# Attention and a gated feed-forward on one core: another start-up list, gate sums out of a projection, and another last tile

## The chip, the core and the metric

One core of a Trainium2 chip runs the program. TensorE (PE) multiplies matrices and loads the weights for that (PEld), VectorE (DVE), ScalarE (ACT) and GpSimd (POOL) work on vectors, SyncE (SP) issues most transfers. The metric is the time of one execution on the device in microseconds (us).

## What is computed

```python
x = A_x                                   # 1 x 2048 x 512
g = sigmoid((x * gate_w).sum(-1))         # one gate for each token
# attention: 32 heads of 16, one K and one V for all heads
q = (x @ wq) as 32 heads;  k = x @ wk;  v = x @ wv
a = softmax(q k^T / 4) v, heads side by side, @ wo
# feed-forward of width 1792
b = ((x @ w_gate) * (x @ w_up)) @ w_down
out = g * a + (1 - g) * b
```

All is float32. Where a product of 32-bit accuracy is wanted, a matrix is kept as a high and a low part in fp32r, and each product is three matmuls (`mm3`): high by high, low by high, high by low.

## The kernel before

**Units and rounds.** Attention works in 64 units: 128 tokens (a tile `t` of a chunk `c` of 512 tokens) by eight heads (a group `g`). A unit has 16 steps in each of three passes. The first pass (`p1`, L699) multiplies Q by K with the queries on the partitions, and DVE takes the maximum of each row (L700); two matmuls to a step, one for each half of the heads, on the upper and the lower 64 rows of TensorE at the same time (two lanes, LANE = 232 ns in the planner). After the last maximum of a unit, `p1_end` reduces them on DVE (L708 to L714), stores them through DRAM (L720, four transfers) and fetches them as two more rows of the unit's Q tile (L727, two transfers). The second pass (`p2`, L740) needs these rows: it gives the scores less the maximum, transposed, and ACT takes the exponential (L741). The third (`pv`, L753) multiplies by V in four column tiles of 32, and ACT copies the sum out (L757), once for each unit.

**The planner.** The schedule is manual: the order in which Python emits the instructions is the order on each engine, and each engine runs its own in order. A string of 144 letters, `ORDER`, is one round of 16 steps: `a`, `b` issue a `p1` matmul on the two lanes, `c`, `d` a `p2` matmul, `p` two steps of `pv`, and `e`, `f` (36 each) a matmul of a filling job, at twelve to a job, so three jobs a round. The jobs are the Q projections of the groups (`q_jobs`), the feed-forward's products (`ffn_job`, `down_jobs`) and the output projection by `wo` (in `norm`), 198 in all. `APART` is the round used instead where a down-projection job of two feed-forward tiles stands ready; there are two such jobs to a chunk. A class `State` keeps estimated times; `later` and `at` put an action (a DMA, a copy) at an estimated time.

**The front.** Before the rounds stand hand-ordered calls (L766 to L798): `x_trans0` and `x_trans` transpose x by TensorE and split it, `kv` projects K and V (a stationary matrix of 128 columns that holds wk three times and wv), `v_trans` brings V back, one Q projection (chunk 0, group 0) is done, stored (`q_store`, two transfers) and fetched (`q_fetch`, L226, six transfers to a unit). `steps` puts four `p1` steps between them. The gate sums are 16 products on POOL (`gate_sum`, L320), each summed on ACT (L324), planned from the end of the front on. Then comes the lead: until 25 `p1` steps (LEAD) are issued and six jobs (LEADJOBS) are filled, `p1` steps and jobs alternate; then `ORDER` runs 64 times. Of unit 0 all 16 steps come first in `order1`, then unit 1, and so on.

**The end.** After the last `pv`, ACT copies the sum to `osb`; TensorE multiplies three quarters of the last tile by `wo` (nine matmuls, 512 columns); `picks` has built two selecting matrices, and eight matmuls by them (L672) take the sums and the values out of `osb` into one bank; DVE forms the reciprocal (L675) and the product (L677); a split, three more matmuls and one VectorE operation (L354) finish the tile, and one transfer stores it (L367).

Of the kernel before, what the change touches and what calls it, by code (L numbers as in the profile page):

```python
# [48 lines left out]
LEADJOBS = 6  # L49
# [12 lines left out]
SLOT = 1  # L62
HALVES = (slice(0, 64), slice(64, 128))
# [5 lines left out]
def mix_kernel(ctx: ExitStack, tc: tile.TileContext, x, wq, wk, wv, wo, wg, wu, wd, gw, out):  # L69
# [34 lines left out]
    z = consts.tile([128, NC * NT], F32, name="z")  # L104
# [58 lines left out]
    def load_x(c):  # L163
        if c < 2:
            xn = [w512("y", F32, 8) for _ in range(NT)]
        else:
            pairs = [work.tile([128, 2, 512], F32, name="P", tag="P", bufs=PBUF) for _ in range(2)]
            xn = [t[:, i] for t in pairs for i in range(2)]
        for t in range(NT):
            eng = nc.scalar if c == 0 and t == NT - 1 else nc.sync  # L170
            eng.dma_start(xn[t], x2[c * 512 + t * 128:c * 512 + t * 128 + 128, :])
        return xn
# [33 lines left out]
    def q_store(c, g, qh, ql):  # L206
        dq[c, g] = []
        for src in (qh, ql):
            d = dram.tile([128, 512], F32, name="dq", tag="dq", bufs=2 * NC * NG)
            nc.sync.dma_start(d, src.bitcast(F32))  # L210
            dq[c, g].append(d)
        dqat[c, g] = clock["T"] + 4500.0
# [5 lines left out]
    def q_fetch(u):  # L218
        c, g, t = units[u]
        q = Q[u] = work.tile([128, 4, 128], F32R, name="Q", tag="Q", bufs=QB)  # L220
        for d, rows in zip(dq[c, g], ((0, 32), (16,))):
            for half in range(2):
                for r in rows:
                    b = half * 64 + r
                    src = d[half * 64:half * 64 + 64, t * 128:(t + 1) * 128]
                    nc.sync.dma_start(q[b:b + 16].bitcast(F32), src.rearrange("(s d) q -> d s q", d=DH))  # L226
        qat[u] = clock["T"] + 6000.0

    kvn = work.tile([128, 4, 32], F32, name="kvn", tag="oT", bufs=2)
    nc.scalar.dma_start(kvn[:, :, 0:16], wk_v)  # L230
    nc.scalar.dma_start(kvn[:, :, 16:32], wv_v)
    xns = {0: load_x(0)}
    wqn = [stage(wq_v[:, :, 0:128])]
    xns[1] = load_x(1)
    xns[2] = load_x(2)
    xns[3] = load_x(3)
    wqs = [[w512("wh", F32R, WB), w512("wl", F32R, WB)] for g in range(NG)]
    kvs2 = [work.tile([128, 4, 32], F32R, name=n, tag=n, bufs=2) for n in ("rb", "raw")]
# [4 lines left out]
    def kv_split():  # L243
# [8 lines left out]
        split2(*wqs[0], wqn[0])  # L252

    def x_trans0():
        xT[0] = x_tiles()
        hi, lo = xT[0][2:]
        for t in range(NT):
            p = bank(2 + t, "px")
            for k in range(4):
                nc.tensor.transpose(p[:, KS[k]], xns[0][t][:, KS[k]], ident)  # L260
            split(hi[:, :, KS[t]], lo[:, :, KS[t]], p.rearrange("p (k q) -> p k q", k=4))
            if t == 1:
                kv_split()

    def x_trans(c, ks=range(4), pool=()):
        xn = xns[c]
        if c not in xT:
            xT[c] = [[w[:, k] for k in range(4)] for w in (woh, wol)] if c == 3 else \
                x_tiles((("hh", "hl"), ("wdh", "wdl"))[c - 1])
        for k in ks:  # L270
            p = bank(2 + (4 * c + k) % 5, "px")
            for t in range(NT):
                nc.tensor.transpose(p[:, KS[t]], xn[t][:, KS[k]], ident)  # L273
            if k in pool:
                xs = w512(("yt", "osb")[k % 2], F32, 2)
                nc.scalar.copy(xT[c][0][k], p)
                nc.scalar.copy(xs, p)
                nc.gpsimd.tensor_tensor(xT[c][1][k], xs, xT[c][0][k].bitcast(F32), op=OP.subtract)
            else:
                split(xT[c][0][k], xT[c][1][k], p)  # L280

    kvs = {}

    def kv(c, between=None):
        p = ms_bank(c % 2)
# [3 lines left out]
        mm_all(p, prods[:6], True, False)  # L289
        if between:  # L290
            between()
        mm_all(p, prods[6:], False, True)
        Kc = KK[:, c * 512:(c + 1) * 512]
        kvs[c] = w512("gs", F32, 3)
        nc.scalar.activation(Kc, p, AF.Identity, bias=kneg)
        nc.vector.scalar_tensor_tensor(Kc, Kc.bitcast(F32), klow, p, op0=OP.mult, op1=OP.add)
        nc.scalar.copy(kvs[c], p)

    def v_trans(c):
        pv = bank(7, "pv")  # L300
        for t in range(4):
            nc.tensor.transpose(pv[:, t * 128:(t + 1) * 128], kvs[c][:, t * 128:(t + 1) * 128], ident)  # L302
        nc.vector.tensor_copy(V[:, c * 4:(c + 1) * 4, 0:DH].rearrange("p t (h d) -> p t h d", h=2),
                              pv.rearrange("p (t h c) -> p t h c", t=4, h=2)[:, :, :, 50:58])
# [8 lines left out]
    gate_left = [(c, t) for c in (2, 3, 0, 1) for t in range(NT)]  # L313

    def gate_sum():
        if not gate_left:
            return
        c, t = gate_left.pop(0)
        scr = w512("yt", F32, 2)
# [336 lines left out]
    def picks():  # L656
# [4 lines left out]
        for t in sels:  # L661
            nc.gpsimd.memset(t, 0.0)
# [338 lines left out]
```

## Time and profile before

| what | us |
|---|---|
| median of 3 runs (lowest to highest) | 1620.87 (1620.53 to 1621.84) |
| the profiled execution | 1621.27 |
| its span, first to last instruction | 1619.5 |
| PE busy in it | 1610.8 |
| DVE busy | 1381.0 |
| ACT busy | 1245.7 |
| POOL busy | 744.7 |

The granted TensorE clock was 0.999 over the span. Matmuls overlap, so a busy PE is not one at its peak; what bounds a stage is read from what ended the waits there. In a timeline line stand the start, the length, the engine, the line of the kernel, the operation, the tiles written and read, the count, and in brackets the idle time before with what ended it. In the chain of waits stand start, length and what the time went to.

### The profile page before, as it was taken

The page shows a single profiled execution, that of the slowest core. Times are in us where ns is not written, and L with a number is a line of the kernel's source. Part 1 is how long each engine was busy: PE and PEld are TensorE (multiplying, and loading weights), DVE is VectorE, ACT ScalarE, POOL GpSimd, SP SyncE. Part 2 cuts the span into 40 slices and gives each one's busy share as a digit, 9 for nine tenths or more (in the row PEclk, how much of TensorE's full clock was granted, in tenths as well). Part 3 has the DMA queues.
Part 4 walks back from the last instruction along what each step waited for, and adds up shares of the span by engine and source line. Part 5 has one row for each costly group of instructions (what it writes and reads, how often), then busy time and mean ns, then how long its engine had stood idle before and what let it go on. Part 6 is the DMA issues. An engine that isn't in the chain of part 4 may idle for free.

```text
span 1619.5 us, 35319 instructions
## 1 busy us (share of the span) xinstructions
PE 1610.8 (99%) x13126; PEld 1042.4 (64%) x13126; DVE 1381.0 (85%) x2410; ACT 1245.7 (77%) x2411; POOL 744.7 (46%) x876
## 2 busy tenths in 40 slices
PE   9999999999999999999999999999999999999998
PEld 7666666666666666666666666576566666666664
DVE  6988888888898888888888888888888898898870
ACT  4787777777788787787778787787788787787785
POOL 5515652624644642635443651643743641642732
PEclk9999999999999999999999999999999999999999
DMA  4463322212312221212231221222231221222101
GB/s 161 174 212 114 97 67 59 61 54 72 102 58 72 66 73 54 65 52 69 64 100 62 71 66 57 64 59 65 62 111 52 68 79 53 62 65 60 36 25 38
DMA packets 184991, 121.44 MB, mean 75 GB/s; under 512 B 46196, under 2 KB 154356, under 8 KB 184820
## 3 DMA queue, kind: packets, MB, share of 16 engines
q1 hardware_dynamic: 183620, 118.87, 24.5%
q8 instruction: 103, 1.69, 0.4%
q14 instruction: 68, 0.56, 0.1%
q10 hardware_dynamic: 1200, 0.33, 0.1%
HBM read 82.96 MB, written 36.17 MB: 74 GB/s over the span
## 4 chain that ended last, share of the span: by engine, by line
PE 97%; DVE 1%; ACT 1%; issue 0%; POOL 0%; POOLq 0%; ACTq 0%
PE ms L872 34%; PE acc L753 29%; PE s L740 18%; PE s L699 15%; DVE mx L700 1%; PE ms L150 1%; ACT P L741 1%; PE px L273 0%; PE wo L150 0%; PE warm L764 0%; ACT yt L361 0%; PE pv L302 0%; PE pick L672 0%; PE px L260 0%; DVE rb L675 0%
## 5 line engine op out<-in xcount | busy, mean ns | idle before, releaser
L700 DVE TENSOR_REDUCE mx<-s 128x1 f32<-128x512 f32 x2048 | 1306.9, 684 | 171.2 <-PE s L699 87.9
L741 ACT ACTIVATE P<-s 128x512 f32<-128x512 f32 x2048 | 1077.9, 605 | 257.1 <-PE s L740 188.0
L740 PE MATMUL s<-Q,KK 50*128 50x512 f32 x2048 | 750.3, 411 | 0.1
L699 PE MATMUL s<-KK,Q 48*128 48x512 f32 x2048 | 692.7, 407 | 0.1
L753 PE MATMUL acc<-P,V 128*32 128x512 f32 x4096 | 492.9, 598 | 0.0
L740 PEld LDWEIGHTS s<-Q,KK 50*128 50x128 f32 x2048 | 352.6, 185 | 175.6 <-issue 97.2
L699 PEld LDWEIGHTS s<-KK,Q 48*128 48x128 f32 x2048 | 338.6, 185 | 104.0 <-ACT P L741 47.3
L872 PE MATMUL ms<-xh,wh 64*128 64x512 f32 x920 | 338.9, 391 | 0.0
L872 PE MATMUL ms<-xl,wh 64*128 64x512 f32 x920 | 336.5, 391 | 0.0
L872 PE MATMUL ms<-xh,wl 64*128 64x512 f32 x920 | 322.6, 392 | 0.0
L753 PEld LDWEIGHTS acc<-P,V 128*32 128x32 f32 x4096 | 107.9, 109 | 236.2 <-issue 195.4
L535 POOL TENSOR_TENSOR hf<-gs 128x512 f32<-128x512 f32 x56 | 72.0, 1285 | 351.8 <-ACT gs L526 337.0
L362 POOL TENSOR_TENSOR y<-y,yt 128x512 f32<-128x512 f32 x79 | 101.5, 1288 | 233.4 <-ACT yt L361 229.8
L872 PEld LDWEIGHTS ms<-xl,wh 64*128 64x128 f32 x920 | 164.6, 186 | 8.2
L872 PEld LDWEIGHTS ms<-xh,wh 64*128 64x128 f32 x920 | 163.5, 185 | 9.6 <-issue 0.4
L872 PE MATMUL ms<-wdh,hh 64*128 64x512 f32 x448 | 164.6, 393 | 0.0
L872 PE MATMUL ms<-wdl,hh 64*128 64x512 f32 x448 | 164.2, 391 | 0.0
L872 PEld LDWEIGHTS ms<-xh,wl 64*128 64x128 f32 x920 | 157.8, 186 | 9.8 <-issue 0.3
L872 PE MATMUL ms<-wdh,hl 64*128 64x512 f32 x448 | 158.9, 392 | 0.0
L138 POOL TENSOR_TENSOR wl<-wn,wh 128x512 fp32r<-128x512 f32 x116 | 149.5, 1289 | 9.3
L757 ACT COPY osb<-acc 128x512 f32<-128x512 f32 x64 | 37.6, 587 | 75.8 <-PE acc L753 75.8
L635 POOL TENSOR_TENSOR oT<-raw,rb 128x128 f32<-128x128 f32 x63 | 29.1, 463 | 128.3 <-DMA rb<-dr 128.3
(149 smaller groups left out, 1343.4 us busy)
## 6 DMA issues: line engine op xcount, KB each, us to landing
do<-osb SPq DMA_DIRECT2D x63, 256.0 KB
wn<-in_B_w_gate_dram SPq DMA_DIRECT2D x56, 256.0 KB
wn<-in_B_w_up_dram SPq DMA_DIRECT2D x56, 256.0 KB
wdn<-in_B_w_down_dram SPq DMA_DIRECT2D x56, 256.0 KB
Q<-dq SPq DMA_DIRECT2D x384, 32.0 KB
raw<-do SPq DMA_DIRECT2D x252, 32.0 KB
dq<-oh SPq DMA_DIRECT2D x16, 256.0 KB
dq<-ol SPq DMA_DIRECT2D x16, 256.0 KB
```

The costliest lines, as they stand in the source:

```text
L138: nc.gpsimd.tensor_tensor(lo, src, hi.bitcast(F32), op=OP.subtract)
L150: nc.tensor.matmul(p, l, r, start=start and i == 0, stop=stop and i == len(prods) - 1)
L362: nc.gpsimd.tensor_tensor(y[c, t], y[c, t], tmp, op=OP.add)
L535: nc.gpsimd.tensor_tensor(hf, gu[0], gu[1], op=OP.mult)
L635: nc.gpsimd.tensor_tensor(dst, raw[:, 0], rb, op=OP.mult)
L699: nc.tensor.matmul(p, q[r, slot], KK[r, kq * 512:(kq + 1) * 512], start=True, stop=True)
L700: nc.vector.tensor_reduce(mx[u][:, half * 4 + slot, kq:kq + 1], p, axis=AX.X, op=OP.max)
L740: nc.tensor.matmul(p, KK[r, j * 128:(j + 1) * 128], q[r].rearrange("p s q -> p (s q)"), start=True, stop=True)
L741: nc.scalar.activation(P[s][:, half], p, AF.Exp, scale=0.25)
L753: nc.tensor.matmul(acc[u][b:b + 32, :], V[:, j + i], src[:, half], start=(j == 0), stop=(j == NJ - 2))
L757: nc.scalar.copy(osb, acc.pop(u))
L872: nc.tensor.matmul(p, lhs[HALVES[l]], rhs[HALVES[l]], start=(i == 0 and (l == 0 or j.apart)), stop=(end and (l == 1 or j.apart)))
```

## The change

It alters the front, three numbers, one string and the end; `ORDER` stays.

- The front is a list of 115 short words that one loop runs through. A digit pair is a chunk and an index: `D`, `C` load x, `L` loads a part of wq, `T` transposes four blocks, `X` splits them by ACT and DVE, `P` by ACT and POOL, `K` does three of the twelve K and V matmuls of a chunk, `E` evacuates them, `V` transposes V back, `U` evacuates that, `J` does three of the twelve matmuls of a first Q projection, `Z` evacuates it, `M` moves Q of a unit, `W` and `A` split wq, `N` splits wk and wv, and `S` is half a `p1` step. Banks are taken from a queue of free ones.
- The gate's weights become a 33rd column beside wk and wv, so that the K and V projection gives the gate sums; `U` takes their exponential. `gate_sum`, the tile `z` and the load of the weights to all partitions go. Ahead of the list stand the transfer of the weights as 4 x 128, a transpose of them on TensorE and a copy.
- Chunk 0's group 0 is projected in two halves of the columns (`J0`, `J4`), its units 0 and 1 get their Q by transfers from SBUF to SBUF (`q_move`, six to a unit, three of them on ACT's queue); group 1 (`J1`) is projected in the front too. Two Q jobs of chunk 0 are left, LEADJOBS is 5.
- 22 `S` stand in the list: 11 steps. `order1` starts with the first quarter of K for units 0 and 1, then the other three quarters of unit 0, then those of unit 1.
- wq's columns are stored with the four heads of a half innermost (`wq_split`), `q_store` writes six transfers, `q_fetch` reads two.
- `APART` is another string with the same count of each letter.
- The last unit's picks use two selecting matrices of 32 columns, four column tiles each, in two banks. The last tile's `wo` products, its final VectorE operation and its store are in two halves of 256 columns; the last 128 rows of `wo` are loaded once more in another row order and split (`wo_last`).

```diff
-LEADJOBS = 6
+LEADJOBS = 5
+FRONT = """
+D1 D3 T01 X01 D0 L0 D2 T03 T00 T02 A0 C1 X00 X03 J00 J01 N X02 J02 J03 T10 C2 L1 T12 K00 K01 Z0 T11 M0 X12 K02 K03 P10
+T20 X11 C3 E0 T22 T13 X13 L2 K10 T21 W1 P20 V0 U0 W2 T23 X23 K11 K12 S P22 S S X21 K13 T30 X30 K20 L3 S S J10 E1 J11 S
+S M1 S S K21 T32 P32 J12 T33 K22 T31 S S X33 P31 S S K23 E2 J13 V1 K30 U1 S W3 S K31 Z1 J40 K32 S S K33 E3 V2 J41 S S
+S S J42 J43 U2 V3 Z4 S U3
+"""
+FRONTQ = (2, 3)
 APART = (
-    "cbebedefcfebedefcbefedebedefafcfafefcfafefebedebefefcfafcffacfaffcfefafe"
-    "edbeeddeabppbcdadappadcfafcfefefafedebedefefadfecbefebefedafcdppbcbabcpp"
+    "adcdebefefebcfefadefebededefafcfebefcfafefebedebefefcfaffcfafcaffcfefafe"
+    "eddeebdebcppadcbadppdafcfcbefefebcfefadefefebcefadefefefededabppcbabcbpp"
 )
     def q_store(c, g, qh, ql):
...
+        d = dq[c, g] = dram.tile([2, 3, 64, 512], F32, name="dq", tag="dq", bufs=NC * NG)
+        for r, src in enumerate((qh, ql, qh)):
+            for half in range(2):
+                nc.sync.dma_start(d[half, r], src[HALVES[half]].bitcast(F32))
     def q_fetch(u):
...
+        for half in range(2):
+            src = dq[c, g][half, :, :, t * 128:(t + 1) * 128]
+            nc.sync.dma_start(q[half * 64:half * 64 + 48].bitcast(F32), src.rearrange("r (d s) q -> (r d) s q", s=4))
+    gwn = work.tile([128, 128], F32, name="gwn", tag="rb", bufs=2)
+    nc.scalar.dma_start(gwn[0:4], gw.rearrange("(k p) -> k p", p=128))
+            eng.tensor_copy(w[:, :, 0, 58:59], kvs2[v][:, :, 32:33])
+    def v_evac(c):
+        pv = vp.pop(c).rearrange("p (t h c) -> p t h c", t=4, h=2)
+        nc.vector.tensor_copy(V[:, c * 4:(c + 1) * 4, 0:DH].rearrange("p t (h d) -> p t h d", h=2), pv[:, :, :, 50:58])
+        nc.scalar.activation(gb[:, c * NT:(c + 1) * NT], pv[:, :, 0, 58], AF.Exp, scale=-1.0)
+    def q_move(u):
+        qh, ql = qp["s"]
+        Q[u] = work.tile([128, 4, 128], F32R, name="Q", tag="Q", bufs=QB)
+        for r, src in ((0, qh), (32, qh), (16, ql)):
+            for half in range(2):
+                b = half * 64 + r
+                eng = nc.scalar if u == 0 and half else nc.sync
+                eng.dma_start(Q[u][b:b + 16].bitcast(F32), src[HALVES[half], KS[u]].bitcast(F32))
     def o_last(c, g, t, osb):
         def pick():
-            p = bank(5, "pick")
-            for v in (1, 0):
+            ps, po = bank(5, "sums"), bank(4, "pick")
+            for p, sel in ((ps, st["sel"][1]), (po, st["sel"][0])):
                 for s in range(4):
-                    nc.tensor.matmul(p[:, v * 128:v * 128 + 128], st["sel"][v][:, s], osb[:, KS[s]],
-                                     start=(s == 0), stop=(s == 3))
+                    nc.tensor.matmul(p[s * 32:s * 32 + 32, 0:128], sel, osb[:, KS[s]], start=True, stop=True)
...
+    def y_half(c, t, p, i):
+        k = c * NT + t
+        src = y[c, t][:, COLS[i]]
+        nc.vector.scalar_tensor_tensor(src, p, gg[:, k:k + 1], src, op0=OP.mult, op1=OP.add)
+        (nc.sync, nc.scalar)[i].dma_start(out2[k * 128:k * 128 + 128, COLS[i]], src)
-    order1 = [(0, slot, kq) for kq in range(4) for slot in range(4)]
-    order1 += [(u, slot, kq) for u in range(1, NU) for slot in range(4) for kq in range(4)]
+    order1 = [(u, slot, 0) for u in range(2) for slot in range(4)]
+    order1 += [(u, slot, kq) for u in range(2) for kq in range(1, 4) for slot in range(4)]
+    order1 += [(u, slot, kq) for u in range(2, NU) for slot in range(4) for kq in range(4)]
+    nc.tensor.transpose(p[:, 0:4], gwn[0:4], ident[0:4, 0:4])
+    nc.vector.tensor_copy(kvn[:, :, 32], p[:, 0:4])
...
+    for op in FRONT.split():
+        acts[op[0]](*map(int, op[1:]))
+    done //= 2
-    later(2000.0, lambda: v_trans(2))
-    later(6000.0, lambda: v_trans(3))
-    later(0.0, gate_sum)
-    later(100.0, gate_sum)
```

More of the change, by code (lines that the diff above doesn't have):

```diff
@@ L265, in x_trans @@
-    def x_trans(c, ks=range(4), pool=()):
-        xn = xns[c]
-        if c not in xT:
[L268 to L280, printed above, removed]
@@ new lines, in mix_kernel, with x_trans, x_split @@
+    px, kvp, kvs, vp, qp = {}, {}, {}, {}, {}
+    def x_trans(c, k):
+        p = px[c, k] = hold(("x", c, k), "px")
+        for t in range(4):
+            nc.tensor.transpose(p[:, KS[t]], xns[0][k][:, KS[t]] if c == 0 else xns[c][t][:, KS[k]], ident)
+    def x_split(c, k, pool=False):
+        if c not in xT:
+            xT[c] = [[w[:, i] for i in range(4)] for w in (woh, wol)] if c == 3 else \
+                x_tiles(((), ("hh", "hl"), ("wdh", "wdl"))[c])
+        p = px.pop((c, k))
+        if c == 0:
+            split(*[w[:, :, KS[k]] for w in xT[0][2:]], p.rearrange("p (k q) -> p k q", k=4))
+        elif pool:
+            xs = w512(("yt", "osb")[k % 2], F32, 2)
+            nc.scalar.copy(xT[c][0][k], p)
+            nc.scalar.copy(xs, p)
+            nc.gpsimd.tensor_tensor(xT[c][1][k], xs, xT[c][0][k].bitcast(F32), op=OP.subtract)
+        else:
+            split(xT[c][0][k], xT[c][1][k], p)
+        release(("x", c, k))
@@ L545, in evac @@
                     picks()
+                    later(25000.0, wo_last)
         return Job(lambda: proj(W[n][i][0], xT[c]), evac,
@@ L561, in ffn_jobs @@
         for c in range(NC):
-            yield from q_jobs(c, range(c == 0, NG))
+            yield from q_jobs(c, FRONTQ if c == 0 else range(NG))
         pend = None
```

219 lines of the change are left out of this document (101 added, 118 removed).

## The prediction

> **What bounds the kernel now.** The page first. In its part 1 and in the chain that ended last, TensorE holds the span:
>
> ```profile
> PE 1610.8 (99%) x13126; PEld 1042.4 (64%) x13126; DVE 1381.0 (85%) x2410; ACT 1245.7 (77%) x2411; POOL 744.7 (46%) x876
> ...
> PE 97%; DVE 1%; ACT 1%; issue 0%; POOL 0%; POOLq 0%; ACTq 0%
> ```
>
> The 99% says little, since overlapping matmuls count as busy; the chain says that nothing but TensorE's own order ends the waits, but for 1% on DVE and 1% on ACT. Next, where the stages meet. The list of ACT's copies gives one for each unit, so one for each round:
>
> ```profile
> L757 ACT COPY osb<-acc x64: 586/587/591, 84.7 to 1608.9; 128x512 f32<-128x512 f32 x64
> ```
>
> From 84.7 to 1608.9 are 63 rounds of 24.19. Before and after the change the rounds have the same filling: 198 jobs less 6 in the lead, or 197 less 5, are 192, three for each of 64 rounds. So the rounds stay, and three places can move the time: the front with the lead, the few `APART` rounds, and the end. The chain of waits in the first 80 us shows the lead:
>
> ```profile
> 40.32 9.07 DVE mx L700 x15
> ...
> 50.33 9.57 DVE mx L700 x16
> 59.90 0.04 issue
> 59.94 0.50 PE s L699
> ```
>
> Here TensorE isn't the bound: from 40.32 to 59.90 the chain runs through 31 row maxima on DVE, 0.605 us each (9.07 / 15), and the small operations that end unit 0 between the two (40.32 + 9.07 = 49.39 to 50.33, 0.94 us). The first matmul of the second pass, where the rounds begin, waits for DVE to free a bank, not for its maxima:
>
> ```profile
> 58.74 0.18 PEld L740 LDWEIGHTS s<-Q,KK 50*128 50x128 f32 x1 [0.30 <-DVE mx L700]
> ```
>
> The round's second `b` then stands at 59.94 where, at 0.24 a pair (below), 58.98 would do. So the rounds start in effect at 58.74 + 0.96 = 59.7.
>
> **The front, step by step.** The prices, from the chain of waits in the front:
>
> ```profile
> 1.36 3.25 PE warm L764 x14
> ...
> 8.82 5.73 PE ms L150 x24
> 14.56 3.86 PE px L273 x32
> ...
> 27.85 0.42 PE s L699 x2
> ...
> 30.68 1.59 PE ms L150 x6
> ```
>
> A projection's matmul costs 0.239 (5.73 / 24), a transpose 0.12 (3.86 / 32), a pair of half steps 0.42. Warm-up ends at 4.61 and the front at 32.27: 27.7 us. Before, it holds 64 + 8 transposes (8.7), 60 projection matmuls (14.3) and 4 pairs (1.7), 24.7 in all, so 3.0 idle. After: 64 + 16 transposes (9.6); 48 + 12 matmuls of 512 columns (14.3); 24 of 256 columns, at 0.12 to 0.239, taken at 0.13 as they are nearest the transposes' pace if weights and columns are both short (3.1); 11 pairs (4.6). That is 31.6, and with the same 3.0 idle the front ends at 4.61 + 34.6 = 39.2; without any idle at 36.3. As a share (27.7 / 24.7) the idle would be 3.8: 40.1.
>
> DVE must have done the list's 22 half steps by then. They are 13.3 us; beside them behind the first `S` stand three splits and three K corrections, at 0.645 and 0.75, 4.2 (and the V copies, small):
>
> ```profile
> 25.81 1.29 DVE L143 TENSOR_TENSOR wol<-px,woh 128x512 fp32r<-128x512 f32 x2 [1.54 <-ACT woh L142]
> ...
> 28.61 0.75 DVE L296 SCALAR_TENSOR_TENSOR KK<-KK,klow,ms 128x512 fp32r<-128x512 f32 x1 [0.31 <-ACT KK L295]
> ```
>
> Ahead of the first `S` TensorE has 52 transposes, 21 whole and 12 half matmuls, 12.8 us, so it comes at 17.4 to 20.4; with 17.5 on DVE that is 35 to 38. DVE keeps up, and the front is TensorE's.
>
> The lead is where the gain could be lost. Unit 0 now ends with its 20th step instead of its 16th, since four steps of unit 1 stand ahead. So 40 maxima, of which 22 are done at 39.2: 18 more are 10.9, then 0.94: 51.0, against 50.33 before. The chain of maxima goes on through SP:
>
> ```profile
> 50.35 1.34 SPq L720 DMA_DIRECT2D dm<-mt  x4
> ...
> 55.38 0.75 SPq L727 DMA_DIRECT2D Q<-dm  x2
> ```
>
> Between store and fetch lay 5.03 us; one unit's six fetches (L226) and two stores (L210) went between them on SP; the code asks for 3.2 from the store's plan. After the change a unit's fetch is two transfers, but a group's store is six. I take 3.5, between 3.2 and 5.0. Then 0.75 to issue; the landing isn't in the trace, but at 58.74 the data were there, so between 0 and 2.6; I take 1.8. The rounds then start at 51.0 + 3.5 + 0.75 + 1.8 = 57.1. By then the 50 maxima of the lead are over (39.2 + 28 x 0.605 + 0.94 = 57.1), so nothing else is late: what is late next is the maxima's way through DRAM. TensorE's own floor for the lead is five jobs of 12 pairs and 14 pairs of `p1`, 74 x 0.239 = 17.7, 56.9 from 39.2. Gain 59.7 - 57.1 = **2.6**. Ends: 36.3 in the front and 3.2 + 0.75 behind the maxima give 52.1, but TensorE's floor is 36.3 + 17.7 = 54.0 (gain 5.7); 40.1 and 5.0 + 0.75 + 2.6 give 60.3 (a loss of 0.6).
>
> At nothing I cost:
> - the gate sums' way off POOL and ACT: they ran beside DVE's maxima in the lead, and POOL is busy for 46% of the span. Were POOL what Q's splits wait for there, these would come sooner; the chain has neither of them.
> - the gate's weights at the head of TensorE's queue: their transfer is third on ACT's queue, and what they wait from there lies behind the warm-up to 4.61 or comes on top. No row shows it; it goes into the idle 3.0, and without that cover the front ends later by as much as it waits.
> - the stores in six parts, where SP has no other transfer that is due, and `wo_last` (eight transfers, two operations on POOL), one job's time ahead of its use.
>
> **The `APART` rounds.** There are two for each chunk, eight. In the table of stages the first row is one, the second is not:
>
> ```profile
> 496.60:521.00 24.40, 24.40 (x202) 15.90 (x204) 20.82 (x37) 20.31 (x40) 14.32 (x15) 1.00 0.24 70
> 521.00:545.10 24.10, 24.10 (x202) 15.32 (x204) 21.35 (x38) 18.55 (x36) 9.74 (x12) 1.00 0.22 63
> ```
>
> It is 0.3 longer, and ACT has 20.31 to do instead of 18.55: work, which another order of the same letters doesn't remove. Ends: all of it gained (8 x 0.3 = 2.4) or as much lost. Nearest to no change, I take 0.05 a round, **0.4**.
>
> **The end.** After the last `pv`:
>
> ```profile
> 1604.23 0.16 PEld L753 LDWEIGHTS acc<-P,V 128*32 128x32 f32 x8 [0.37 <-issue]
> 1604.23 1.92 PE L753 MATMUL acc<-P,V 128*32 128x512 f32 x16
> ...
> 1608.75 0.19 PEld L150 LDWEIGHTS wo<-woh,oh 128*128 128x128 f32 x1 [0.84 <-issue]
> ...
> 1608.87 0.59 ACT L757 COPY osb<-acc 128x512 f32<-128x512 f32 x1 [1.15 <-PE acc L753]
> ...
> 1610.93 1.95 PE L672 MATMUL pick<-osb,wn 128*128 128x128 f32 x16
> 1612.91 0.96 DVE L675 RECIPROCAL rb<-pick 128x128 f32<-128x128 f32 x1 [10.51 <-PE pick L672]
> ...
> 1614.58 0.50 PE L150 MATMUL wo<-woh,oh 128*128 128x512 f32 x1 [1.71 <-ACT oh L142]
> ...
> 1615.68 0.75 DVE L354 SCALAR_TENSOR_TENSOR y<-wo,gg,y 128x512 f32<-128x512 f32 x1 [0.83 <-PE wo L150]
> ```
>
> Now only half of the nine matmuls' columns stands ahead of the picks: 1608.75 + 9 x 0.13 = 1609.9 (at 0.239: 1610.9), later than the copy to `osb` (1609.46). Into the picks comes a change to column tiles, 0.37 by the first row. The reciprocal waits for the four matmuls of the sums alone, in a bank of their own: `pv`'s 16 of 512 columns took 1.92, so four tiles run together; the sums are between a quarter of that pace (0.1) and half of the old picks (0.98), taken at 0.3. With 0.3 for the result to reach DVE it starts at 1610.9 instead of 1612.91: 2.0. The change back (0.84 before L150) and the other half of the nine lie beside the 1.65 from 1612.91 to 1614.58. Then three matmuls and 0.75 become three of half the width, 0.44, and 0.44 again: from 1614.58, 0.9 + 0.88 against 1.85, 0.1. From 1616.43 to the span's end (1619.48) is the store, 3.05; half the bytes on each of two queues, between nothing and half: nearest to nothing, as no row shows a store's time to go by its size, 0.2. In all **2.3**; ends 0.6 (whole pace, picks at 0.98) and 3.6.
>
> [...]
>
> **Sum.** 2.6 + 0.4 + 2.3 = 5.3. From the profiled 1621.27 that is 1615.97; the median of the runs is 0.40 below the profiled one, so **1615.6**. A measurement of this kernel can tell about 0.2%, 3.2 us, from no change: 1617.6 and 1624.1 are the marks.
>
> **Rivals.**
> - *The maxima's way takes the front's gain.* Unit 0's chain ends no sooner than before (51.0 against 50.33), and SP's order decides. If fetch and landing are as slow as the upper ends, the rounds start at 59.7 and 2.7 are left: 1618.2, no change that can be told. For it: 5.03 in the trace. Against: nothing else needs SP then that can't be two transfers.
> - *The list flows without idle.* Front over at 36.3, the rest as above: 54.2, 5.5 gained, and 0.4 and 2.3, and 1.0 more from the open end of `APART`: 1620.87 - 9.2 = 1611.7. For it: the new list puts work of another chunk between a product and its use; against: 3.0 idle before.
> - *SP blocked by stores: slower.* SP runs in order, and a store whose POOL part isn't ready holds the fetch of the maxima behind it:
>
> ```profile
> SPq L210 <- ACT oh L343: 6.5, 2, 4.6
> ```
>
>   Thirty stores are issued in the lead instead of twelve. One such wait of 4.6 ahead of unit 0's fetch makes 1620.2; a second, ahead of the Q of unit 2, which the 33rd step needs, makes 1624.8. It decides from the point where SP's fetch comes over 8.5 us later than forecast. Against: POOL, freed of the gate sums, has the low parts sooner.
>
> **Chances.** Forecast 0.45 (its own range 1613 to 1617.6); no idle 0.20; the maxima's way 0.23; blocked 0.12. Faster 0.65, same 0.23, slower 0.12. The range leaves out most of the blocked case and the ends beyond the no-idle case: 1610 to 1621.5.
>
> **What would show it.** Right: the first L740 at 56 to 58 with a wait for the DMA of the maxima, not for DVE; the first L757 copy near 82; 63 rounds of 24.2; the reciprocal's start 2 us nearer to the last `pv`. The front is wrong if the first job's matmul (L872 before) comes after 41 or unit 0's L714 after 53; the rounds are wrong if their mean leaves 24.15 to 24.23.

## The result and the profile after

The changed kernel takes 1630.4 us (median of 6 runs, 1629.21 to 1632.18) against 1620.72 for the kernel before on the same chip: a ratio of 1.0059 (95% interval 1.0046 to 1.0072). It is slower by 9.7, where 5.3 faster was forecast. The profiled execution took 1629.51 with a span of 1627.7, 8.2 more than the span before.

The page of the changed kernel, parts 1 and 4 (busy time of the engines, then the chain that ended last by engine and by line):

```profile
PE 1614.4 (99%) x13139; PEld 1046.3 (64%) x13139; DVE 1381.5 (85%) x2411; ACT 1238.1 (76%) x2388; POOL 730.0 (45%) x857
...
PE 94%; ACT 1%; DVE 1%; SPq 1%; DMA 1%; issue 1%; POOL 0%; ACTq 0%; DVEq 0%; POOLq 0%
PE ms L912 33%; PE acc L807 29%; PE s L794 17%; PE s L753 14%; SPq L223 1%; DVE mx L754 1%; ACT P L795 1%; DMA dq<-oh 1%; PE kv L158 1%; PE q L158 0%; DMA y<-in_A_x_dram 0%; PE px L282 0%; POOL ol L371 0%; ACT oh L370 0%; ACT yt L391 0%
```

TensorE has fallen from 97% of the chain to 94%, and two names are in it that weren't there: SP's issue of the stores (L223) and the transfer that they start (`dq<-oh`). ACT copies one unit's sum in each round, so these copies mark the rounds (kernel after, the copy's own line):

```profile
L811 ACT COPY osb<-acc x64: 586/587/591, 87.6 to 1619.9; 128x512 f32<-128x512 f32 x64
```

Before it ran from 84.72 to 1608.87, now from 87.61 to 1619.87. The table sorts the 8.2 by these copies:

| stretch | before | after | difference |
|---|---|---|---|
| start to the first copy | 84.72 | 87.61 | +2.89 |
| first round after it | 24.52 | 28.42 | +3.90 |
| second | 24.49 | 28.22 | +3.73 |
| the other 61 rounds | 1475.14 | 1475.62 | +0.48 |
| last copy to the span's end | 10.63 | 7.83 | -2.80 |

So the loss is over by 145 us, and the end gains what was expected of it. The 2.89 of the first stretch isn't the stores' alone: with two whole stores 1.66 of it stays (86.38 for the first copy, below). What SP issues in that time stands in the lines of the stores; the columns are the shortest, median and longest issue in ns and the first and last start. Kernel after:

```profile
L223 SPq DMA_DIRECT2D dq<-oh x64: 445/595/746, 36.7 to 159.2; - x64
L223 SPq DMA_DIRECT2D dq<-ol x32: 445/587/1890, 38.1 to 157.9; - x32
```

Kernel before:

```profile
L210 SPq DMA_DIRECT2D dq<-oh x16: 319/358/501, 15.2 to 140.1; - x16
L210 SPq DMA_DIRECT2D dq<-ol x16: 319/340/404, 15.9 to 141.5; - x16
```

A store of 64 rows holds SP for 0.59, one of 128 rows held it for 0.35. Six for two makes 3.6 for a group where 0.7 was: 96 x 0.59 = 57 us of SP against 32 x 0.35 = 11, all of it in the first 160 us. The four transfers to a unit that the change saves for this (two fetches for six) are spread over the whole kernel. SP's timeline around unit 0's maxima (`dm` stores, then the fetch `Q<-dm`), before:

```profile
54.48 0.37 SPq L210 DMA_DIRECT2D dq<-oh  x1
54.95 0.38 SPq L210 DMA_DIRECT2D dq<-ol  x1
55.38 0.75 SPq L727 DMA_DIRECT2D Q<-dm  x2
```

and after:

```profile
54.98 1.50 SPq L774 DMA_DIRECT2D dm<-mt  x4
56.57 1.10 SPq L223 DMA_DIRECT2D dq<-oh  x2
57.77 1.19 SPq L223 DMA_DIRECT2D dq<-ol  x2
59.01 1.25 SPq L223 DMA_DIRECT2D dq<-oh  x2
60.36 0.68 SPq L781 DMA_DIRECT2D Q<-dm  x2
```

SP has no gap there: one group's six stores fill the 3.8 us ahead of the fetch. Who waits for them (the table of waits after: total, times, longest; none of these three rows stands in that of before):

```profile
ACT oh L370 <- DMA dq<-oh: 7.1, 4, 3.3
...
PEld s L794 <- DMA Q<-dm: 3.8, 2, 2.9
...
PE s L794 <- DMA Q<-dm: 3.1, 2, 2.0
```

And the chain of waits after, at the start of the rounds:

```profile
59.01 0.60 SPq L223
59.66 2.41 DMA dq<-oh
62.25 0.63 ACT oh L370
62.95 1.30 POOL ol L371
64.29 1.11 SPq L223
65.44 0.60 SPq L223
66.04 0.43 issue
66.47 2.23 DMA dq<-oh
68.80 0.62 ACT oh L370
69.42 0.50 ACT P L795
```

This is a ring. ACT's cast into `oh` needs one of two buffers, so it waits until the store of two groups earlier has read it; that store is late in SP's queue. Behind the cast on ACT, which runs in order, stand the exponentials (L795), and behind these the rounds. The first full round loses time in the same way (TensorE idle for 1.58 before 108.55, behind ACT's exponentials), the second by the fetch of a unit's maxima, which SP issues too late (idle for 2.02 before 117.99).

Behind such a wait TensorE's granted clock fell as well. In the table of windows stand the window, its length, the busy time of PE, PEld, DVE, ACT and POOL with counts, then the granted clock, the share of the DMA engines and GB/s (kernel after):

```profile
110.50:113.90 3.40, 3.40 (x18) 1.04 (x10) 1.50 (x3) 0.51 (x2) 0.00 (x0) 0.50 0.78 206
```

The kernel before has no such stretch in its rounds. At half the clock 3.4 us of work take up to 1.7 more than they need (an estimate from this row), so of the 3.90 that the first full round lost a part is the clock and not the wait itself.

### The profile page after: what moved, and what is told of

Read it like the earlier page. It is cut to its first block, busy times and chain, and to the rows that moved or that the text cites. A ratio compares the mean times of both kernels' runs of the same rounds, so it can differ in the third digit from the quotient of the medians.

```text
span 1627.7 us, 35116 instructions
## 1 busy us (share of the span) xinstructions
PE 1614.4 (99%) x13139; PEld 1046.3 (64%) x13139; DVE 1381.5 (85%) x2411; ACT 1238.1 (76%) x2388; POOL 730.0 (45%) x857
## 4 chain that ended last, share of the span: by engine, by line
PE 94%; ACT 1%; DVE 1%; SPq 1%; DMA 1%; issue 1%; POOL 0%; ACTq 0%; DVEq 0%; POOLq 0%
PE ms L912 33%; PE acc L807 29%; PE s L794 17%; PE s L753 14%; SPq L223 1%; DVE mx L754 1%; ACT P L795 1%; DMA dq<-oh 1%; PE kv L158 1%; PE q L158 0%; DMA y<-in_A_x_dram 0%; PE px L282 0%; POOL ol L371 0%; ACT oh L370 0%; ACT yt L391 0%
## 5 line engine op out<-in xcount | busy, mean ns | idle before, releaser
L795 ACT ACTIVATE P<-s 128x512 f32<-128x512 f32 x2048 | 1078.1, 605 | 257.1 <-PE s L794 177.9
L912 PE MATMUL ms<-xh,wh 64*128 64x512 f32 x912 | 336.4, 392 | 0.0
L912 PE MATMUL ms<-xl,wh 64*128 64x512 f32 x912 | 334.9, 391 | 0.0
L912 PE MATMUL ms<-xh,wl 64*128 64x512 f32 x912 | 319.7, 391 | 0.0
L912 PEld LDWEIGHTS ms<-xl,wh 64*128 64x128 f32 x912 | 163.4, 186 | 8.5
L912 PEld LDWEIGHTS ms<-xh,wh 64*128 64x128 f32 x912 | 161.9, 185 | 9.3
L912 PE MATMUL ms<-wdh,hh 64*128 64x512 f32 x448 | 164.9, 393 | 0.0
L912 PE MATMUL ms<-wdl,hh 64*128 64x512 f32 x448 | 164.3, 391 | 0.0
L912 PEld LDWEIGHTS ms<-xh,wl 64*128 64x128 f32 x912 | 156.4, 186 | 9.9
L912 PE MATMUL ms<-wdh,hl 64*128 64x512 f32 x448 | 158.8, 392 | 0.0
```

The costliest lines, as they stand in the source:

```text
L795: nc.scalar.activation(P[s][:, half], p, AF.Exp, scale=0.25)
L912: nc.tensor.matmul(p, lhs[HALVES[l]], rhs[HALVES[l]], start=(i == 0 and (l == 0 or j.apart)), stop=(end and (l == 1 or j.apart)))
```

## The experiments

All ratios are to the kernel before on the same chip, whose median was 1621.48, 1621.21, 1621.48 and 1621.53 in the four groups of runs. Theory: the time that SP needs to issue the six-part stores makes the loss. Rivals: the new front itself is late; or what lands slowly is the half store, not its issue.

**Three stores for six** (changed kernel, each store one transfer over both halves):

```diff
-            for half in range(2):
-                nc.sync.dma_start(d[half, r], src[HALVES[half]].bitcast(F32))
+            nc.sync.dma_start(d[:, r], src.bitcast(F32))
```

> The changed kernel with three whole stores of 128 rows for a group's Q in place of six half stores; all else stays. Theory S (SP's queue of stores holds ACT's next Q copy and the fetch of the maxima): the rounds 1 and 2, 28.4 and 28.2 us, fall to 24.5 to 25.5, the first L757-like copy of a sum moves from 87.6 to about 86, the time falls by 6 to 9 us to 1621 to 1624. Rival F (the new front and its fewer leading jobs make the rounds long): rounds 1 and 2 stay near 28, time within 1.5 us of 1630.

Measured: 1800.4, ratio 1.1103 (1.1087 to 1.1120). No theory had that. A wait and a step of the chain of this kernel:

```profile
ACT oh L369 <- DMA dq<-oh: 121.6, 11, 22.0
```

```profile
99.88 18.41 DMA dq<-oh
```

One store, with the half as outermost dimension, of size 2, now takes 18.4 us to land (another in the chain 18.5), where that of the changed kernel took 2.4. The landing by itself is that much slower, so the run says nothing on the number of issues. Why it is slower, no run here shows.

**Two whole stores, six fetches** (changed kernel with two whole stores to a group and six fetches to a unit, as before; its other parts kept; called the two-store kernel from here on):

```diff
-        d = dq[c, g] = dram.tile([2, 3, 64, 512], F32, name="dq", tag="dq", bufs=NC * NG)
-        for r, src in enumerate((qh, ql, qh)):
-            for half in range(2):
-                nc.sync.dma_start(d[half, r], src[HALVES[half]].bitcast(F32))
+        d = dq[c, g] = dram.tile([2, 128, 512], F32, name="dq", tag="dq", bufs=NC * NG)
+        for v, src in enumerate((qh, ql)):
+            nc.sync.dma_start(d[v], src.bitcast(F32))
...
+            for r, v in ((0, 0), (16, 1), (32, 0)):
+                b = half * 64 + r
+                src = dq[c, g][v, HALVES[half], t * 128:(t + 1) * 128]
+                nc.sync.dma_start(q[b:b + 16].bitcast(F32), src.rearrange("(d s) q -> d s q", s=4))
```

> The changed kernel with the store and the fetch counted as before: two whole stores to a group, six fetches to a unit; wq's new column order stays. Theory S: rounds 1 and 2 at 24.5 to 25.5, time 1621 to 1625. If it is the number of all SP transfers and not the stores (rival), this has 26 for a group where the changed kernel has 14, and should be as slow as it or slower, 1630 or more.

Measured: 1620.77, ratio 0.9995 (0.9986 to 1.0005); the first copy at 86.38, the next rounds 24.51 and 24.59, as the theory had it. Its SP timeline at the same place:

```profile
54.28 1.45 SPq L775 DMA_DIRECT2D dm<-mt  x4
55.83 0.35 SPq L222 DMA_DIRECT2D dq<-oh  x1
56.28 0.38 SPq L222 DMA_DIRECT2D dq<-ol  x1
57.06 0.56 SPq L782 DMA_DIRECT2D Q<-dm  x2
```

The fetch is out 2.8 after the maxima's store, and the waits for `dq<-oh` and `Q<-dm` are gone. The six-part layout costs 9 us (spans of 1627.7 and 1618.7), the whole of the loss. The number of transfers alone isn't the cause, since a unit's fetch is six transfers again here; they only stand elsewhere. It also leaves the new front later than the old: 86.38 against 84.72.

**The stores alone** (kernel before, with the order of wq's columns, the six stores and the two fetches of the changed kernel):

```diff
+        d = dq[c, g] = dram.tile([2, 3, 64, 512], F32, name="dq", tag="dq", bufs=NC * NG)
+        for r, src in enumerate((qh, ql, qh)):
+            for half in range(2):
+                nc.sync.dma_start(d[half, r], src[HALVES[half]].bitcast(F32))
...
-        split2(*wqs[g], wqn[g])
+        wq_split(g)
```

> The kernel before with only the new Q layout: wq's columns reordered, six half stores to a group, two fetches to a unit. Theory S: rounds 1 and 2 grow from 24.5 to 27 to 28.5 and the time by 5 to 9 us, to 1626 to 1630. Rival F: no growth, 1620 to 1622.

Measured: 1636.26, ratio 1.0088 (1.0073 to 1.0103). Its waits have the row that those of before lack:

```profile
ACT oh L343 <- DMA dq<-oh: 8.4, 3, 4.7
```

So the old front loses 14.8 by the same edit, more than the 5 to 9 expected; the new front isn't needed for it. The first copy came at 90.32, the next rounds took 30.80 and 26.18. Some 3.4 of this the changed kernel doesn't share: here the Q of unit 0 goes through the six stores too, and unit 0's reduction ended at 53.70 where it had ended at 50.33. The granted clock was 0.50 for 10.2 us in the first rounds.

**Whole stores and other transfers in SP's way** (two whole stores, and behind each group's four small constant ones):

```diff
+        for _ in range(4):
+            e = dram.tile([64, 128], F32, name="pad", tag="pad", bufs=4)
+            nc.sync.dma_start(e, ident[0:64, :])
```

> The kernel with two whole stores and six fetches (1620.8), and behind the two stores of each group four small transfers of a constant (64 rows of 512 bytes) that nobody waits for: SP again has six transfers to a group. If SP's issue time in the first 150 us is the cause: rounds 1 and 2 at 26.5 to 28.5, time 1626 to 1630. If it is how the half stores land (their shape, half as many bytes more), the pads cost nothing: within 1 us of 1620.8.

Measured: 1637.63, ratio 1.0104 (1.0089 to 1.0119); the first copy at 87.89, then rounds of 27.81 and 35.16. The constants take 0.60 to issue, like a half store (2.41 for four in SP's timeline), and the waits are back:

```profile
PEld s L798 <- DMA Q<-dm: 13.4, 4, 8.8
PE s L798 <- DMA Q<-dm: 10.8, 3, 7.9
...
ACT oh L374 <- DMA dq<-oh: 2.8, 2, 2.2
```

Nobody waits for the constants, and the stores of Q are whole; they only stand in SP's queue. By the sums of the rows of SP's timelines, SP was issuing for 50.0 of the 53 us from 57 to 110 here, 50.4 in the changed kernel, 49.7 in that with the stores alone, 42.2 with two whole stores and 35.8 before: of these five the three slow kernels are those in which SP is full. So SP's time is enough to make a loss of this kind, and the shape in which a half store lands isn't needed for it. The size of this loss measures more than SP's time: in the second round TensorE waited 7.9 for the maxima, and when it went on at 123.5 the granted clock stood at 0.50 until 129.5, which is up to 3.0 us of the 10.7 that this round lost (an estimate). The DMA engines aren't short either, by the window's row; before they were at 0.62 and 220:

```profile
57.00:110.00 53.00, 49.49 (x391) 33.88 (x389) 42.07 (x73) 39.77 (x76) 10.20 (x10) 1.00 0.53 182
```

**The end alone** (kernel before with the new `o_last`, `wo_last` and halves of the last tile, as in the change):

```diff
-            p = bank(5, "pick")
-            for v in (1, 0):
+            ps, po = bank(5, "sums"), bank(4, "pick")
+            for p, sel in ((ps, st["sel"][1]), (po, st["sel"][0])):
...
-                    nc.tensor.matmul(p[:, v * 128:v * 128 + 128], st["sel"][v][:, s], osb[:, KS[s]],
-                                     start=(s == 0), stop=(s == 3))
+                    nc.tensor.matmul(p[s * 32:s * 32 + 32, 0:128], sel, osb[:, KS[s]], start=True, stop=True)
```

> The kernel before with only the new end: picks in column tiles, last tile in halves. The traces of both kernels put the end at 10.6 and 7.8 us behind the last copy of a sum, so 2.8 us less: 1618. If a shorter end were paid for by the second load and split of wo's last rows, nothing: 1620.7.

Measured: 1619.15, ratio 0.9985 (0.9976 to 0.9994). Its median is the lowest of all. The gain is 2.3, less than 0.2%, but its interval lies under 1.

**Unit 0 first, x earlier.** The start of the new front was 1.7 late even with whole stores. The first theory for this was unit 0's chain of maxima, in which four steps of unit 1 now stand:

```diff
-    order1 = [(u, slot, 0) for u in range(2) for slot in range(4)]
-    order1 += [(u, slot, kq) for u in range(2) for kq in range(1, 4) for slot in range(4)]
+    order1 = [(u, slot, kq) for u in range(2) for kq in range(4) for slot in range(4)]
```

> The kernel with two whole stores and six fetches, and all 16 steps of unit 0 ahead of unit 1 again. Its first copy of a sum came at 86.4, before the change at 84.7. Theory: unit 0's maxima end late (54.25 against 50.33) because four steps of unit 1 stand ahead of them; eight maxima less put them at 49.4, the first copy at 84 to 85 and the time at 1618.5 to 1619.5. Rival: the lead's 50 maxima or its jobs hold the rounds anyway, first copy at 86 to 87, time as it was.

Measured: 1626.18, ratio 1.0034 (1.0021 to 1.0047). Unit 0's maxima were reduced 3.0 sooner (50.35 for 53.35), and yet the first copy came at 91.94, 5.6 later: the planner put two of its own waiting steps (`fence`, TensorE waits for DVE) into the lead. TensorE was idle for 1.74 before the first of them ended, and the granted clock was 0.50 from 61.2 to 64.6. So the forecast was missed, but the theory isn't decided: the edit changed the order of the lead too, and that took more than unit 0's chain gained.

The second was the tile of x that the second transposition waits for. Tile 3 goes by SP and tile 2 by ACT, and the gate's weights are transposed behind the third transposition:

```diff
-        (nc.scalar if t == NT - 1 else nc.sync).dma_start(xns[0][t], x2[t * 128:t * 128 + 128, :])
+        (nc.scalar if t == 2 else nc.sync).dma_start(xns[0][t], x2[t * 128:t * 128 + 128, :])
...
-D1 D3 T01 X01 D0 L0 D2 T03 T00 T02 A0 C1 X00 X03 J00 J01
+D1 D3 T01 X01 D0 L0 D2 T03 T00 T02 G A0 C1 X00 X03 J00 J01
```

> The kernel with two whole stores and six fetches; tile 3 of x is loaded through SP and tile 2 behind the gate's weights on ACT's queue, and the transpose of those weights stands behind the first four tiles. TensorE's first transposes came at 5.63 and 7.54, before the change at 4.40. Theory: the front is late as a whole by this, so it starts 1.2 earlier and the first copy comes at 84.5 to 85.5, time 1619 to 1620. Rival: the splits of wq and the Q transfers on ACT's queue hold it anyway, first copy within 0.5 of 86.4.

Measured: 1624.33, ratio 1.0019 (1.0010 to 1.0029). ACT issued tile 2 only at 5.50, behind its first cast, and the fourth transposition waited 4.24 for it: the edit delayed the front where it was to speed it up. Behind this wait the granted clock was 0.50 from 9.4 to 19.7. The two together came through whole: unit 0's reduction and the first copy were 5.5 and 5.6 later. Both edits together:

> Both edits on the kernel with two whole stores and six fetches. If unit 0's maxima hold the start of the rounds, the two add up until the 50 maxima of the lead hold it: first copy at 82.5 to 84, time 1617 to 1618.5. If either was hidden by the other, 1619.

Measured: 1630.28, ratio 1.0057 (1.0042 to 1.0072), the first copy at 96.30: both delays are in it, the waiting steps and the slow head, and it says no more than the two runs before.

**All of x by SP; unit 0's Q by SP; both; the old `APART`.** Each has two whole stores and one edit: no first tile of x on ACT's queue (and the gate's weights behind the third transposition); no `q_move` on ACT's queue; both; the old string.

```diff
-        (nc.scalar if t == NT - 1 else nc.sync).dma_start(xns[0][t], x2[t * 128:t * 128 + 128, :])
+        nc.sync.dma_start(xns[0][t], x2[t * 128:t * 128 + 128, :])
...
-                eng = nc.scalar if u == 0 and half else nc.sync
-                eng.dma_start(Q[u][b:b + 16].bitcast(F32), src[HALVES[half], KS[u]].bitcast(F32))
+                nc.sync.dma_start(Q[u][b:b + 16].bitcast(F32), src[HALVES[half], KS[u]].bitcast(F32))
```

> Two whole stores and six fetches as in two_stores_six_fetches (1620.77), but all four first tiles of x are loaded by SP (none behind ACT's work) and the transpose of the gate weights goes out after the third transposition instead of ahead of everything. Theory A (the delay at the head of the front is passed on to the rounds one for one, as the late tile of x_tile_early was): the second transposition of the list no longer waits 1.26 us for a tile and the first no longer waits behind the gate weights; first osb copy 85.0 to 85.6 instead of 86.38, time 1619.5 to 1620.2. Theory B (the start of the rounds is held by what the list does later, the split of the query weights and ACT's 2.4 us of DMA issues at 12.8): first copy within 0.4 of 86.38, time within 0.5 of 1620.8.

> two_stores_six_fetches, but the copies that gather the query of unit 0 are all issued by SP instead of half by ACT, which was held for 2.4 us behind its issues at 12.8. Theory A (ACT's evacuations behind these issues are the front's limit there): first copy 84.0 to 85.5, time 1618.4 to 1620. Theory B (SP's queue then holds the later of the copies about as long, or ACT has slack): first copy 86 to 87.5, time 1620.4 to 1622.

> Both of the two before: all first tiles of x and all copies of unit 0's query by SP. If both Theory A hold, first copy 83.2 to 84.8 and time 1617.5 to 1619.3, below the 1619.15 of the new end alone, so the front would then gain by itself; if Theory B holds of one, the time is that of the other alone; if of both, 1620.3 to 1621.5.

> two_stores_six_fetches with the old written order for the eight rounds that run apart. By the sums of those rounds in the two traces the new order gives 0.25 us: time 1620.7 to 1621.3. If the new order gave the 0.4 that the prediction took, 1621.1 to 1621.4; if it gives nothing, 1620.5 to 1620.9.

Measured: 1621.11 (0.9996, 0.9987 to 1.0005), 1621.83 (1.0002, 0.9993 to 1.0011), 1622.29 (1.0007, 0.9998 to 1.0015) and 1621.41 (0.9998, 0.9989 to 1.0007), the first copies at 86.74, 87.09, 87.67 and 87.59. The first three miss what the theory of the delays promised, and the third is later than both its parts. The last can't decide: its rounds take 1524.85 from first copy to last, against 1524.49 with the new string, but the five kernels with the new string and whole stores beside it and in the next part spread from 1524.78 to 1525.72. What it showed was something else, and it bears on the other three too. Its front is instruction for instruction that of the two-store kernel, and its first copy came 1.2 later. TensorE's timeline has the reason (start, length; the half matmuls of the first Q projection), in this kernel:

```profile
11.71 0.41 PE L158 MATMUL q<-xh,wl 128*128 128x256 f32 x1
11.92 0.41 PE L158 MATMUL q<-xl,wh 128*128 128x256 f32 x1
```

in the two-store kernel:

```profile
11.27 0.28 PE L158 MATMUL q<-xh,wl 128*128 128x256 f32 x1
11.39 0.28 PE L158 MATMUL q<-xl,wh 128*128 128x256 f32 x1
```

They come every 0.21 us in the one and every 0.12 in the other. In the kernel with all of x by SP the transposes were done sooner, but then the granted clock fell (table of windows):

```profile
9.80:13.00 3.20, 3.15 (x15) 3.15 (x16) 2.68 (x9) 0.37 (x1) 1.08 (x4) 0.50 0.97 330
```

The first half matmul started at 8.14 there, for 10.21 in the two-store kernel, the last at 11.94 for 12.11: two waits and half the clock took back nearly all that x had gained.

**TensorE kept busy at the head.** Transposes that nobody reads go into the idle places of the two-store kernel (and, in the same way, of that with all of x by SP); the kernel before loses eight of its 14 warm-up transposes, to make the gap there.

```diff
-    for i in range(14):
+    for i in range(20):
         nc.tensor.transpose(p[:, KS[i % 4]], ident, ident)
...
+    def keep(n):
+        f = bank(7, "keep")
+        for i in range(n):
+            nc.tensor.transpose(f[:, KS[i % 4]], ident, ident)
...
-D1 D3 T01 X01 D0 L0 D2 T03 T00 T02 A0 C1 X00 X03 J00 J01
+D1 D3 T01 X01 D0 L0 D2 F5 T03 T00 T02 A0 C1 X00 X03 F2 J00 J01
```

> two_stores_six_fetches (1620.8, first copy 86.38 and 87.59 in two profiles of this front) with 13 more transposes on TensorE that nobody reads: six behind the warm-up, five behind the first transposition of x, two ahead of the first query projection. Clock theory (the gaps at the head keep TensorE at half its clock until 10 to 13 us): the half matmuls of the first query projection come at 0.12 from the start, the first copy at 84.5 to 85.5, time 1618.5 to 1619.8. List theory (the middle of the list holds the front, whatever the head does): first copy 86 to 87.6, time 1620.4 to 1621.8.

> x_all_by_sp (1621.1, first copy 86.74, granted clock 0.50 from 9.8 to 13 us) with 12 such transposes: four ahead of the third transposition, eight ahead of the first query projection. Clock theory: clock 1.00 from 5 us on, the first query projection done at 10.5 to 11 instead of 12.2, first copy 84.5 to 85.5, time 1618.8 to 1619.9. List theory: first copy 86.2 to 87.6, time 1620.6 to 1621.8.

> The kernel before with 6 warm-up transposes instead of 14: TensorE is idle from 2.8 to 4.4 us. Clock theory: the transposes of x and the first projections run at half the clock for about 3 us, the first copy comes 1 to 2 us later (85.7 to 86.7), time 1622 to 1623.3. List theory (for that front too the head has slack): first copy 84.4 to 85, time 1621 to 1621.7.

Measured: 1619.81 (0.9990, 0.9981 to 0.9999), 1620.11 (0.9990, 0.9981 to 0.9999) and 1621.46 (1.0004, 0.9995 to 1.0012). The first copies came at 85.29 and 86.11. The half matmuls come at 0.12 from the fourth on (10.35 in the first kernel, 10.47 in the second), and the window that was at half the clock is at the full one; the second of these kernels:

```profile
9.80:13.00 3.20, 2.99 (x22) 2.71 (x23) 3.17 (x10) 0.38 (x1) 1.09 (x4) 1.00 1.00 343
```

So TensorE's pace at the head was about 1 us of the start's lateness, by medians too (0.71 under the kernel before without the transposes, 1.72 with them; 0.37 and 1.42 in the other pair). The second stays short of its forecast, 85.5 at most; the runs also lie closer together (1619.58 to 1620.64, against 1619.56 to 1621.81 without the transposes). The third misses in its median, but not in every execution: its 11 runs reach from 1621.08 to 1625.49, and in the profiled one, which is that of 1625.49, the first copy came at 88.09 and the first eight projection matmuls, from 9.39 on, every 0.44 (0.24 in the kernel before). So with the gap the start was slow in this execution, and by the times not in all. And what the new front should gain stays out at the full pace too: 85.29 is still later than 84.72.

## Why the prediction was wrong

**The step that failed** is "the stores in six parts, where SP has no other transfer that is due", costed at nothing. All of Q's groups are stored in the first 160 us, where x is stored, the maxima are fetched and two units' Q as well: in the kernel before SP was already issuing for 35.8 of the 53 us from 57 to 110. A price was at hand in the prediction's own rows: SP issues the maxima's transfers at 0.34 and 0.38 each, so four more stores for a group are some 1.4 even at that pace. The real pace for half the rows was 0.59, and the excess 2.9 for a group. In the sum the stores stand in the 3.5 from the reduction's end to the fetch: it measured 6.1 (54.26 to 60.36), with whole stores 2.8. The greater part was in no term at all, because of "So the rounds stay": the first two full rounds lost 7.6. The two-store kernel shows the step as a difference of 9 us, the six stores in the kernel before as one of up to 14.8, and the constants show that transfers which only fill SP's queue do it.

**The rival that happened** was "SP blocked by stores: slower", with 0.12. Its sign and place were right, its mechanism only in part. It had SP waiting for POOL's low part, with a row that shows a wait for ACT's high part (`ACT oh L343`), so the row doesn't carry it; and in the changed kernel SP waited for POOL's low parts for 0.8 in all between 48 and 150 us. SP was held by the issues, and the new waits were ACT's, for its buffer, and TensorE's, for the maxima. "POOL, freed of the gate sums" was no argument against that. What the changed kernel would have had to show for it, a fetch "over 8.5 us later than forecast", was also wrong: unit 0's fetch was issued at 60.36, 5.9 after the 54.5 of the forecast (51.0 + 3.5), and the rest was lost in the two rounds after it.

**The front's end.** Forecast 39.2, with 41 as the mark: the first job's matmul (L912) came at 40.56, so not wrong by its mark, and 1.4 late. "It goes into the idle 3.0", said of the gate's weights, was short: their wait left 0.87 idle, and the next, for a tile of x, 1.26, and from 8.2 to 11.4 TensorE's transposes and half matmuls came every 0.21 where 0.11 and 0.12 is the full pace (granted clock 0.50).

**"DVE keeps up."** It didn't. The table of DVE's timeline in the changed kernel, from 31 us to unit 0's reduction:

```profile
31.13 1.29 DVE L754 TENSOR_REDUCE mx<-s 128x1 f32<-128x512 f32 x2 [1.60 <-PE s L753]
...
36.94 1.29 DVE L754 TENSOR_REDUCE mx<-s 128x1 f32<-128x512 f32 x2 [0.74 <-PE s L753]
38.55 0.75 DVE L312 SCALAR_TENSOR_TENSOR KK<-KK,klow,kv 128x512 fp32r<-128x512 f32 x1 [0.33 <-ACT KK L311]
39.22 2.48 DVE L754 TENSOR_REDUCE mx<-s 128x1 f32<-128x512 f32 x4
...
42.47 10.84 DVE L754 TENSOR_REDUCE mx<-s 128x1 f32<-128x512 f32 x18
53.35 0.19 DVE L762 TENSOR_REDUCE mm<-mx 128x8 f32<-128x32 f32 x1
```

The first `S` was at 21.68 and not at 17.4 to 20.4; DVE then waited for scores, and had 17 of the 22 maxima done at 39.2. Five more at 0.605 are 3.0: the reduction ended at 54.26 instead of 51.0, past the mark of 53. That the whole 3.3 comes from there is read from this trace; no run isolates it. With the credit below it is the whole difference between the first copy that the forecast implies (84.72 - 2.6 = 82.1) and the 86.38 of the two-store kernel.

**The maxima's way.** With whole stores it took what was forecast: 6.0 from the reduction's end (54.26) to the first matmul of the second pass (60.29), against 6.1 (51.0 to 57.1). With the six stores that matmul came at 62.23, and for the reason named, the transfer of the maxima:

```profile
62.23 0.47 PE L794 MATMUL s<-Q,KK 50*128 50x512 f32 x1 [1.11 <-DMA Q<-dm]
```

Not there was the credit of 0.96 that I took for the second matmul: from the first matmul to the first copy were 25.98 before (58.74 to 84.72) and 26.09 in the two-store kernel (60.29 to 86.38).

**`APART`** was taken at 0.4. The eight rounds differ by 0.25 in the two traces; whether that is its gain stays open. **The rounds** were wrong by their own mark, 24.15 to 24.23: their mean was 24.32 (87.61 to 1619.87). All of it is in the first two; the other 61 changed by 0.48 in all.

**The end** was right, in size and in its steps: 2.3 forecast, 2.8 by the traces, 2.3 by the end alone. The changed kernel's last copy, picks and reciprocal:

```profile
1619.87 0.59 ACT L811 COPY osb<-acc 128x512 f32<-128x512 f32 x1 [1.15 <-PE acc L807]
...
1620.98 0.43 PE L709 MATMUL sums<-osb,sel 128*32 128x128 f32 x8
1621.22 0.40 PE L709 MATMUL pick<-osb,sel 128*32 128x128 f32 x8
1621.47 0.96 DVE L711 RECIPROCAL rb<-sums 128x128 f32<-128x128 f32 x1 [8.02 <-PE sums L709]
```

From the copy to the reciprocal are 1.60, before 4.04: 2.4 for the 2.0 taken. That 2.0 has in it 0.3 for the result to reach DVE, an estimate of mine that no run shows by itself; from the first matmul of the sums to the reciprocal it took 0.49 (1620.98 to 1621.47), for the 0.6 taken with the matmuls. The store gave the rest: 2.73 from the end of the last VectorE operation to the span's end, before 3.05, so 0.3 for the 0.2 taken.

## What to carry to other kernels

A transfer had two prices here: the time until it landed (2.4 us for a half store in the changed kernel's chain), and the time in which the queue that issues it issued nothing else (0.59 for a half store, 0.35 for a whole one). Sum the second by stage, not over the kernel, and count every transfer that the stage has already; an edit that saves issues all along a kernel and spends them in its first tenth can lose, as this one lost 9 us. A buffer that a store reads ties its next writer to the store's place in the queue, so a late queue stops an engine that never waits for the queue itself: ACT's casts waited 7.1 us for the stores in the changed kernel. And a short wait of TensorE can cost more than its length, when the granted clock falls behind it: after the wait of 1.58 it stood at 0.50 for 3.4, up to 1.7 more by the estimate above.

## What the runs showed of the hardware

- A store of 64 rows took SP longer to issue (0.59) than one of 128 rows of the same length (0.35). Why, no run here says.
- A store whose outermost dimension has size 2 took 18.4 us to land, for 2.4 with the halves as transfers of their own. Why, no run here says.
- TensorE started at half its pace in the profiles of the kernel before and of the changed kernel (warm-up transposes every 0.21 us, later ones every 0.11). The kernel before reached the full pace at 6.3. With the new front's idle places at the head (0.87 and 1.26 in the changed kernel, 0.83 and 0.99 in that with the old `APART`) TensorE had the full pace at 11.3 in one profiled execution of the two-store front (the lines of the two-store kernel above), and still half of it at 13.0 in another of the same front; in the changed kernel it had it by 5.8 and lost it again from 8.2 to 11.4. With 13 idle transposes in these places four transposes of x took 0.66 from 5.71 on, for 1.12 from 5.64 without them. The granted clock showed the loss (0.50 from 8.2 to 11.4) but stood at 1.00 through the slow starts, where only the matmuls' spacing told. Why the pace was half at the start, and why it was lost again in the changed kernel, no run here shows.
- In the rounds the granted clock fell to 0.50 in the three kernels with a full SP queue, for 3.4 us in the changed kernel and 10.2 in each of the two others, near waits of TensorE of 1.5 to 7.9 us. Other waits of 2.0 there were not followed by it.
